# A state-space mixer with a token MLP: eight rows of x in a place of their own, loaded early, and a new order

## Chip, cores, metric

One core of a Trainium2 chip runs the whole program. The metric is the device time of one execution in microseconds; the time of before is the median of three runs. The engines are PE (matmuls), DVE and ACT (elementwise work and evictions of PSUM), POOL (small elementwise work, and transfers issued by software), SP (issues transfers). They run their own queues in order and wait for each other through semaphores.

## What is computed

The input x is `A_q`, with 2048 positions (S) and 448 channels (D). A position is split as 16 q + r, so that each of 128 partitions q holds 16 "rows" r.

```python
h  = x + A(layernorm(x), A_k, A_v, shift_k, ssm_k, ssm_D)
h2 = h + B(layernorm(h), w1, b1, w2, b2)
# A: kv = causal 4-tap filter of k along S, times v
#    y  = causal convolution of kv with ssm_k along S (FFT of length 2 S) + kv * ssm_D
#    returns layernorm(x) * y
# B: token MLP: LayerNorm again, then along S: gelu(h^T w1 + b1) w2 + b2
```

## The kernel before

The FFTs are built as two matmul stages with a shuffle in between. Everything is listed ahead of time: the emitting functions record operations, and the table `ORDER` says in which order each engine's queue takes them. An operation is named by tag, step and number: `u1.8:0-7` are the eight matmuls of the step u1.8, `u1.8:8` its eviction, 9 to 11 its shuffle transfers. The scheduler puts the waits in, and it picks the PSUM banks and ring slots by itself, the one that it reckons free first.

The stages in order of time:

- Tables, loads of the filter k, of v and of `A_k`, then the filter stage: `kv` (short filter, multiplied into V at L998 on DVE), `k1` and `u1` (first FFT stage of filter and of kv, L1050). Four steps make a group. Each step is evicted from two PSUM banks by ACT or DVE (L1058, L1060) into one of four ring slots; transfers shuffle a pair of steps into TK or TU (L1066: two on POOL, one on SP).
- `k2` and `u2` (second stage, L1085), evicted in place into TK and TU (L729 to L733).
- `i1`: 16 products on DVE (L1152, 1792 elements each), which need all shuffles landed because they write where ring slots 0 and 1 lie; matmuls (L1169), evictions (L729) and shuffles into TZ (L1193; the last step's at L1180).
- `ct`: transposes of a table (L1099). `i2`: for each row r two matmuls (L1292) and, for rows 0 and 1, four more that read TU in place (L1300). Rows 0 to 3 are combined with a normalised x that `xn` makes (L1262); the others are first evicted by a gate (L1309 on ACT, L1311 on DVE) and then combined (L1319). The combination of rows 0 to 3 is L1329.
- The second LayerNorm: statistics of the combined rows (L1335, L1338 for rows 0 and 1, squares on ACT at L1347 and sums for the others), POOL's small steps (L1357 to L1367) and its power (L1371), and the normalised row on DVE (L1378), which is the MLP's input.
- `mlp`: seven accumulations over the 16 rows (L1425), seven more with the other half of w1 (L1435), gelu (L1415), then 16 rows of 14 matmuls with w2 (L1447), sums on DVE (L1450) and stores.

The statistics of x for the first LayerNorm (`q`) are a BN statistic and an aggregate on DVE for each row (L1229, L1231) and an add and a power on POOL for two or four rows (L1237, L1240). q.1 holds rows 0 and 1, q.2 rows 2 and 3, and so on to q.8. x is loaded by four transfers of four rows (`xload`, L906, 448 KB each) into the place of ring slots 2 and 3:

```python
o_GR = (o_WR, o_WR + 8 * DB, o_X, o_X + 8 * DB)
```

so all four wait until every u shuffle has landed (`after=shuf["u"]`). On SP they stand behind the zero fill of TZ (`ct0.1:0`, L1109), which waits for POOL's memset of EW (L1125).

Of the kernel before, what the change touches and what calls it, by code (L numbers as in the profile page):

```python
# [7 lines left out]
ALU = mybir.AluOpType  # L8
# [71 lines left out]
    ),  # L80
# [8 lines left out]
    ),  # L89
}  # L90

def _hpush(h, item):
    h.append(item)
    i = len(h) - 1
    while i > 0:
        parent = (i - 1) >> 1
# [1413 lines left out]
```

## Time and profile before

| | |
|---|---|
| median of 3 runs | 173.48 us (173.15 to 174.06) |
| the profiled execution | 173.96 us, of which the span is 172.1 |
| PE busy | 161.1 us (94%), 1419 matmuls |
| DVE busy | 103.0 us (60%) |
| ACT busy | 89.5 us (52%) |
| POOL busy | 59.6 us (35%) |
| moved by DMA | 35.15 MB, mean 204 GB/s |

An engine's line gives its busy time; in section 2 of the page each digit is the busy tenth of a 4.3 us slice. DVE has 6 to 9 tenths in the first 20 slices and at most 3 in the last 10. The granted TensorE clock is full in every slice. Rows of the timeline give start, time, engine, line, operation, and in brackets the idle time ahead of it with what ended it. Rows of neighbouring operations overlap by up to a tenth of a microsecond, so lengths do not add up to the time from the first start to the last end.

### The profile page before, as it was taken

The numbers are of one execution on the slowest core, as the hardware profiler recorded it, in microseconds if no ns is written. First come the engines' busy times: TensorE is split into PE (matmuls) and PEld (weight loads), VectorE is DVE, ScalarE is ACT, GpSimd is POOL, SyncE is SP. The second block draws the span as 40 slices with busy tenths as digits, with TensorE's granted clock in tenths as the row PEclk, the third lists the DMA queues.
The fourth block names the chain that finished last, engine by engine and source line by source line (L and its number), as shares of the span: only waits on it lengthen the run. The fifth ranks groups of instructions, "written<-read, shape, count | busy, mean of one in ns | idle before, by whom it ended". The sixth has DMA issues, their size and how long they took to land.

```text
span 172.1 us, 3566 instructions
## 1 busy us (share of the span) xinstructions
PE 161.1 (94%) x1419; PEld 92.6 (54%) x1419; DVE 103.0 (60%) x191; ACT 89.5 (52%) x129; POOL 59.6 (35%) x154
## 2 busy tenths in 40 slices
PE   6999999989989988877999999999999999999994
PEld 2776745442333332433445555555567777777783
DVE  7998999868979999989897750000003132132231
ACT  3696757799999999889874447321210000000000
POOL 8346718681902524495889630000000000000000
PEclk9999999999999999999999999999999999999999
DMA  5999866792849985557999999920000111101111
GB/s 176 396 299 388 279 187 238 297 340 96 262 108 372 335 262 181 149 159 247 391 400 404 418 421 422 422 85 0 0 0 4 53 53 53 53 0 57 53 53 53
DMA packets 15404, 35.15 MB, mean 204 GB/s; under 512 B 3756, under 2 KB 9500, under 8 KB 15388
## 3 DMA queue, kind: packets, MB, share of 16 engines
q1 hardware_dynamic: 12300, 28.29, 45.3%
q0 software_dynamic: 2944, 6.55, 11.7%
q8 instruction: 11, 0.18, 0.4%
q10 hardware_dynamic: 144, 0.08, 0.2%
q14 instruction: 5, 0.04, 0.1%
HBM read 22.05 MB, written 1.84 MB: 139 GB/s over the span
## 4 chain that ended last, share of the span: by engine, by line
PE 60%; DVE 15%; DMA 10%; POOL 5%; ACT 4%; issue 2%; SPq 1%; DVEq 0%; ACTq 0%; POOLq 0%
PE ps L1447 24%; PE ps L1435 12%; PE ps L1425 12%; DVE arena L1152 9%; DMA arena<-arena 5%; DMA arena<-in_A_ssm_k_dram 5%; POOL arena L1066 3%; ACT arena L1060 3%; PE ps L1050 3%; DVE arena L1229 2%; PE ps L983 2%; PE ps L1085 2%; PE ps L1029 2%; PE ps L1292 1%; PE ps L957 1%
## 5 line engine op out<-in xcount | busy, mean ns | idle before, releaser
L1450 DVE SCALAR_TENSOR_TENSOR arena<-ps,arena 128x448 bf16<-128x448 f32 (+2 forms) x17 | 11.1, 656 | 55.7 <-PE ps L1447 55.7
L1447 PE MATMUL ps<-arena 128*128 128x448 bf16 (+2 forms) x238 | 42.7, 342 | 0.0
L1447 PEld LDWEIGHTS ps<-arena 128*128 128x128 bf16 x238 | 33.3, 145 | 9.5
L729 ACT CAST arena<-ps 128x896 bf16<-128x896 f32 (+1 forms) x31 | 24.9, 949 | 1.0 <-DVE arena L1231 0.3
L1425 PE MATMUL ps<-arena 128*128 128x448 bf16 x112 | 23.0, 353 | 1.2 <-DVE arena L1367 0.9
L1060 ACT CAST arena<-ps 128x896 bf16<-128x896 f32 x23 | 19.5, 913 | 6.0 <-PE ps L1050 5.4
L1066 POOL DMA_DIRECT2D arena<-arena x32 | 17.6, 553 | 12.5 <-ACT arena L1060 11.9
L1435 PE MATMUL ps<-arena 128*128 128x448 bf16 x112 | 21.7, 352 | 0.0
L1085 PE MATMUL ps<-arena 128*64 128x448 bf16 x128 | 15.8, 360 | 2.0 <-ACT arena L1060 0.9
L1415 ACT ACTIVATE arena<-ps,arena 128x448 bf16<-128x448 f32 x14 | 8.2, 639 | 17.5 <-PE ps L1435 15.1
L1152 DVE TENSOR_TENSOR arena<-arena 128x1792 bf16<-128x1792 bf16 x16 | 16.6, 1082 | 1.1 <-DMA arena<-arena 1.1
L1425 PEld LDWEIGHTS ps<-arena 128*128 128x128 bf16 x112 | 10.6, 98 | 12.3 <-DVE arena L1378 1.8
L1435 PEld LDWEIGHTS ps<-arena 128*128 128x128 bf16 x112 | 11.0, 98 | 10.2
L1169 PE MATMUL ps<-arena 64*128 64x448 bf16 x128 | 14.4, 351 | 1.9 <-DVE arena L1152 1.2
L1050 PE MATMUL ps<-arena 128*32 128x448 bf16 x256 | 14.8, 355 | 0.3
L1193 POOL DMA_DIRECT2D arena<-arena x15 | 8.7, 585 | 15.8 <-ACT arena L729 15.8
L1347 ACT ACTIVATE arena<-arena 128x448 bf16<-128x448 f32 x14 | 8.0, 575 | 7.0 <-DVE arena L1319 6.8
L1085 PEld LDWEIGHTS ps<-arena 128*64 128x64 f16 x128 | 5.4, 108 | 11.5 <-ACT arena L729 3.8
L1169 PEld LDWEIGHTS ps<-arena 64*128 64x128 f16 x128 | 5.1, 94 | 11.0 <-ACT arena L729 5.3
L732 DVE COPY arena<-ps 128x1024 bf16<-128x1024 bf16 (+2 forms) x15 | 9.2, 649 | 0.6 <-PE ps L1029 0.6
L1229 DVE BATCH_NORM_STATS2 arena<-arena 128x6 f32<-128x448 bf16 x16 | 9.3, 612 | 0.0
L1050 PEld LDWEIGHTS ps<-arena 128*32 128x32 f16 x256 | 5.1, 95 | 7.8 <-DVE arena L998 1.9
(97 smaller groups left out, 189.7 us busy)
## 6 DMA issues: line engine op xcount, KB each, us to landing
arena<-in_B_w_dram SPq DMA_DIRECT2D x8, 896.0 KB, 10.2
arena<-in_B_w_dram SPq DMA_DIRECT2D x2, 2048.0 KB, 17.3
arena<-arena SPq DMA_DIRECT2D x16, 224.0 KB, 3.4
arena<-arena POOLq DMA_DIRECT2D x32, 112.0 KB, 3.4
arena<-in_B_w_dram SPq DMA_DIRECT2D x2, 1536.0 KB, 19.3
arena<-arena POOLq DMA_DIRECT2D x14, 196.0 KB, 5.2
arena<-in_A_k_dram SPq DMA_DIRECT2D x4, 448.0 KB, 5.9
arena<-in_A_v_dram SPq DMA_DIRECT2D x4, 448.0 KB, 8.7
```

The costliest lines, as they stand in the source:

```text
L729: return e.copy(out=dst(), in_=src())
L1050: op("pe", lambda e, W, b=b, r=r, q=q, x=x, c0=c0: e.matmul(PS[32 * q:32 * q + 32, b.slots[x], 0:D], E[:, 2 * r + x, c0:c0 + 32], src[:, r ...
L1060: return e.copy(out=dst, in_=Ppair(b)) if W == "act" else e.tensor_copy(out=dst, in_=Ppair(b))
L1066: shuf[tag].append(op(q_, lambda e, W, g=g, i=i, a=a, nu=nu, jh=jh: e.dma_start(T[a + i:a + i + 4 * nu - 3:4].rearrange("p (j k) c d -> p ...
L1085: op("pe", lambda e, W, b=bs[h], h=h, j=j, c=c, par=par: e.matmul(PS[64 * par:64 * par + 64, b.slots[c], 0:D], FW[:, 64 * c:64 * c + 64], ...
L1152: op("dve", lambda e, W, m=m, i=i: e.tensor_tensor(out=MR(m.slots[0]).rearrange("p (x y) d -> p x y d", x=2), in0=TU[:, i].unsqueeze(2).br ...
L1169: k = op("pe", lambda e, W, b=bs[h], m=ms[h], par=par, t=t, tab=tab, xy=xy, P=P: e.matmul(Pb(b, par), tab[P, :], MR(m.slots[0])[P, xy, :], ...
L1229: op("dve", lambda e, W, bs=bs, r=r: e.bn_stats(out=bs, in_=X[:, r, :]), r=[(o_X + r * DB, DB)], w=[(ob, 24)], n=D, kind="1x")
L1425: op("pe", lambda e, W, r=r, fc=fc, b=bs[fc]: e.matmul(Pb(b), W1A[:, r, 128 * fc:128 * fc + 128], Q[:, r, :], start=(r == 0), stop=(r == R ...
L1435: op("pe", lambda e, W, r=r, fc=fc, b=b: e.matmul(Pb(b), W1B[:, r, 128 * (fc - n0):128 * (fc - n0) + 128], Q[:, r, :], start=(r == 0), sto ...
L1447: op("pe", lambda e, W, r=r, fc=fc, b=b, d0=d0, d1=d1: e.matmul(Pb(b)[:, d0:d1], W2[fc // 7][:, fc % 7, r:S:R], G[:, fc, d0:d1], start=(fc ...
L1450: op("dve", lambda e, W, r=r, b=b, A=A, d0=d0, d1=d1: e.scalar_tensor_tensor(out=X[:, r, d0:d1], in0=Pb(b)[:, d0:d1], scalar=bm[:, r:r + 1 ...
```

## The change

Rows 0 to 7 of x get a place of their own (XA, 7168 bytes in each partition at the end of the arena); rows 8 to 15 stay where ring slot 3 lies (XB). The small area shrinks from 4096 to 4032 bytes. The two loads of rows 0 to 7 no longer wait for the u shuffles and are issued on SP behind the fourth k shuffle; the other two follow after the last u shuffle, as before. The four in-place matmuls of rows 0 and 1 (L1300) come before their two other matmuls (L1292) in the accumulation. The tables `ORDER` for all engines are new, and PSUM banks and ring slots are no longer picked but written down (`SLOTS`).

```diff
-    NSMALL = 4096
+    NSMALL = 4032
...
-        TOT = SMALL + NSMALL
+        o_XA = SMALL + NSMALL
+        TOT = o_XA + 8 * DB
...
-        X = view(o_X, [R, D])
+        XA = view(o_XA, [8, D])
+        XB = view(o_X + 8 * DB, [8, D])
+        X2 = lambda r, n: (XA if r < 8 else XB)[:, r % 8:r % 8 + n]
+        XR = lambda r: (XA if r < 8 else XB)[:, r % 8, :]
+        oX = lambda r: o_XA + r * DB if r < 8 else o_X + r * DB
...
         def emit_xload():
             for c in range(4):
-                op("sp", lambda e, W, c=c: e.dma_start(X[:, 4 * c:4 * c + 4, :], x2d[:, 4 * c:4 * c + 4, :]),
-                   w=[(o_X + 4 * c * DB, 4 * DB)], dmab=128 * 4 * DB,
-                   after=shuf["u"])
+                op("sp", lambda e, W, c=c: e.dma_start(X2(4 * c, 4), x2d[:, 4 * c:4 * c + 4, :]),
+                   w=[(oX(4 * c), 4 * DB)], dmab=128 * 4 * DB, after=shuf["u"] if c > 1 else ())
...
-                    for h in range(2):
-                        k = op("pe", ... Pb(b), ET[:, 2 * r + h, :], TZ[:, r, h, :], start=(h == 0), stop=(h == 1 and r >= NZ)) ...
                     if r < NZ:
-                        sch.t0 += 0.2
                         for h in range(2):
                             for jx in range(2):
...
+                                    Pb(b), EW[:, 4 * r + 2 * jx + h, :], TU[:, j, h, :], start=(h == 0 and jx == 0), stop=False),
...
+                        sch.t0 += 0.2
+                    for h in range(2):
+                        k = op("pe", ... Pb(b), ET[:, 2 * r + h, :], TZ[:, r, h, :], start=(h == 0 and r >= NZ), stop=(h == 1)) ...
...
+SLOTS = (
+        ... k1.7:0:6 u1.7:0:2 u1.8:0:4 u1.9:0:6 u1.8:8:3 k1.3:0:4 k2.0:0:0 k2.1:0:6 k2.12:0:2 k2.13:0:4 ...
+)
...
         def can_acquire(o):
...
+            return all(turn[b.pool, i][0] is b and b.pool.free_t[i] <= t + 1e-6 for b in o.acq for i in b.slots)
```

A SLOTS entry is step, operation and bank (or slot): k1.3 gets the pair of banks 4 and 5 that u1.8 had; before it had the pair of k1.7.

What moves in the queues, in the parts that the prediction speaks of (DVE and SP from the diff, shortened to the span):

```diff
 dve:
-k1.0:8 k1.1:8 u1.3:8 kv.13:28-29 kv.14:24-25 k1.2:8 kv.15:28-29 u1.7:8 k1.3:8 k2.1:5 k2.5:4 kv.16:24-25 k2.9:5 u1.10:8 u1.11:8 k2.3:4 k2.7:4 k2.11:4 k2.15:5 u2.13:5
+k1.0:8 k1.1:8 q.2:0 kv.13:28-29 q.2:2 kv.14:24-25 q.2:3 q.2:1 q.4:2 k1.2:8 q.4:3 q.1:2 kv.15:28 q.1:0 kv.15:29 q.1:1 u1.9:8 k1.3:8 k2.1:5 k2.13:5 q.4:0 kv.16:24-25 k2.9:5 u1.12:8 q.4:1 q.1:3 q.3:2 u1.15:8 k2.3:4 k2.7:4 k2.11:5 k2.15:4 u2.13:5 u2.1:5
-i1.0:0 i1.1:0 i1.14:0 i1.13:0 i1.7:0 i1.8:0 i1.10:0 i1.9:0 q.1:0 q.1:2 q.1:1 q.2:0 q.3:0 i1.11:0 i1.12:0 ct0.0:8 q.3:1 i1.5:0 q.5:0 i1.6:0 q.5:1 u2.3:4 i1.3:0 i1.2:0 q.7:0 i1.15:0 i1.16:0
+i1.0:0 i1.1:0 i1.14:0 i1.13:0 i1.8:0 i1.7:0 xn.3:1 i1.9:0 i1.10:0 u2.11:4 q.3:0 i1.11:0 q.3:1 i1.12:0 ct0.0:8 i1.5:0 i1.6:0 i1.3:0 i1.6:9 i1.2:0 i1.16:0 i1.15:0
+q.6:2 q.3:3 q.5:0 q.6:3 q.5:2 xn.0:1 q.8:2 q.5:3 q.6:0 q.5:1 q.6:1 q.7:2 q.8:0 q.8:3 ct.0:8 q.8:1 i2.3:0 i2.11:0 i2.4:0 i2.12:0 i2.5:0 i2.13:0 i2.6:0 i2.14:0 i2.18:0 i2.21:0 i2.8:0 i2.34:0 i2.29:0 i2.16:0
 sp:
+... k1.13:11 k1.15:11 xload.0:0 xload.1:0 u1.1:11 ... u1.15:11 ct0.1:0 xload.2:0 xload.3:0 w1a.0:0 ...
 pool:
+... k1.3:9 q.2:4 k1.3:10 ... u1.11:10 ew.0:1-2 q.1:4 ew.0:3 q.1:5 ew.0:0 q.2:5 xn.0:0 xn.3:0 i1.1:19 ...
 pe:
+... i1.16:10-17 i1.16:1-8 warm.0:0 ct.0:0-7 ct.1:0-7 ct.2:0-7 i2.9:0-3 i2.1:0-3 warm.1:0 i2.2:0-1 i2.10:0-1 i2.45:0-1 ...
```

(i2.1 and i2.9 are the in-place matmuls of rows 0 and 1, i2.2 and i2.10 their other two; i2.3 and i2.11 their combinations, i2.8 and i2.16 their normalised rows.) ACT takes u1.3, u1.7, u1.10 and u1.11 and gives u1.9, u1.12 and u1.15 to DVE; its u1.7 now stands behind u1.8. In the MLP the single matmuls of rows 4 to 15 are interleaved in another way, and three of the w1 second-half accumulations (mlp.19, mlp.20, mlp.21) start between the last rows instead of mlp.17 alone. The rest of ORDER is new in the same sense, and names of x in L1229, L1262, L1319, L1450 and the stores follow the new place.

More of the change, by code (lines that the diff above doesn't have):

```diff
@@ L358, in schedule @@
         INF = 1e18
-        def can_acquire(o):
-            need = {}
-            for b in o.acq:
-                need[b.pool] = need.get(b.pool, 0) + b.k
-            for p, k in need.items():
-                if pick(p, k) is None:
-                    return False
-            return True
-        def pick(p, k):
-            ok = [x <= t + 1e-6 for x in p.free_t]
-            if k == 1:
-                best = None
-                for i in range(p.n):
-                    if ok[i]:
-                        key = (p.pairs and ok[i ^ 1], p.free_t[i], i)
-                        if best is None or key < best:
-                            best = key
-                return None if best is None else [best[2]]
-            best = None
-            for i in range(0, p.n, 2):
-                if ok[i] and ok[i + 1]:
-                    key = (max(p.free_t[i], p.free_t[i + 1]), i)
-                    if best is None or key < best:
-                        best = key
-            return None if best is None else [best[1], best[1] + 1]
+        turn = {}
+        for token in SLOTS.split():
+            step, k, i = token.split(":")
+            (b,) = ops[steps[step][int(k)]].acq
+            b.slots = [int(i) + x for x in range(b.k)]
+            for x in b.slots:
+                turn.setdefault((b.pool, x), []).append(b)
+        def can_acquire(o):
+            return all(turn[b.pool, i][0] is b and b.pool.free_t[i] <= t + 1e-6 for b in o.acq for i in b.slots)
         while done < n:
@@ L399, in schedule @@
                         p = b.pool
-                        b.slots = pick(p, b.k)
                         for i in b.slots:
+                            turn[p, i].pop(0)
                             b.extra.extend(p.prev[i])
@@ L1228, in emit_q @@
                     bs = view(ob, [6], f32)
-                    op("dve", lambda e, W, bs=bs, r=r: e.bn_stats(out=bs, in_=X[:, r, :]), r=[(o_X + r * DB, DB)],
+                    op("dve", lambda e, W, bs=bs, r=r: e.bn_stats(out=bs, in_=XR(r)), r=[(oX(r), DB)],
                        w=[(ob, 24)], n=D, kind="1x")
@@ L1261, in norm @@
                         if W == "act":
-                            return e.activation(out=XN[:, r, :], in_=X[:, r, :], func=ACT.Identity, bias=qx[:, r, 1:2],
+                            return e.activation(out=XN[:, r, :], in_=XR(r), func=ACT.Identity, bias=qx[:, r, 1:2],
                                                 scale=qs[:, r, 3:4])
-                        return e.tensor_scalar(out=XN[:, r, :], in0=X[:, r, :], scalar1=qs[:, r, 0:1],
+                        return e.tensor_scalar(out=XN[:, r, :], in0=XR(r), scalar1=qs[:, r, 0:1],
                                                scalar2=qs[:, r, 3:4], op0=ALU.subtract, op1=ALU.mult)
-                    op(FX, norm, r=[(o_X + r * DB, DB), (o_qst + 16 * r, 16), (o_qx + 8 * r, 8)],
+                    op(FX, norm, r=[(oX(r), DB), (o_qst + 16 * r, 16), (o_qx + 8 * r, 8)],
                        w=[(o_TK + r * 4 * D, 4 * D)], n=D, est={"act": 664.0, "dve": 430.0})
@@ L1290, in emit_i2 @@
                     tz = [(o_TZ + r * 2 * DB, 2 * DB)]
-                    for h in range(2):
-                        k = op("pe", lambda e, W, b=b, r=r, h=h: e.matmul(
-                            Pb(b), ET[:, 2 * r + h, :], TZ[:, r, h, :], start=(h == 0), stop=(h == 1 and r >= NZ)),
-                           r=[r_ET(r)] + tz, bw=[b], n=D, after=av[-1:] if r >= 8 and h == 0 else ())
                     if r < NZ:
-                        sch.t0 += 0.2
                         for h in range(2):
@@ L1300, in emit_i2 @@
                                 k = op("pe", lambda e, W, b=b, r=r, h=h, j=j, jx=jx: e.matmul(
-                                    Pb(b), EW[:, 4 * r + 2 * jx + h, :], TU[:, j, h, :], start=False, stop=(h == 1 and jx == 1)),
-                                   r=[(o_EW + 1024 * r + 512 * jx + 256 * h, 256), (o_TU + (2 * j + h) * DB, DB)], bw=[b], n=D, safter=(k,))
+                                    Pb(b), EW[:, 4 * r + 2 * jx + h, :], TU[:, j, h, :], start=(h == 0 and jx == 0), stop=False),
+                                   r=[(o_EW + 1024 * r + 512 * jx + 256 * h, 256), (o_TU + (2 * j + h) * DB, DB)], bw=[b], n=D,
+                                   safter=(k,) if h + jx else ())
+                        sch.t0 += 0.2
+                    for h in range(2):
+                        k = op("pe", lambda e, W, b=b, r=r, h=h: e.matmul(
+                            Pb(b), ET[:, 2 * r + h, :], TZ[:, r, h, :], start=(h == 0 and r >= NZ), stop=(h == 1)),
+                           r=[r_ET(r)] + tz, bw=[b], n=D, after=av[-1:] if r >= 8 and h == 0 else (),
+                           safter=(k,) if r < NZ else ())
                     i2_last.append(k)
@@ L1318, in comb @@
                     def comb(e, W, r=r, A=A, acc=None):
-                        return e.scalar_tensor_tensor(out=A, in0=X[:, r, :], scalar=qs[:, r, 0:1], in1=A,
+                        return e.scalar_tensor_tensor(out=A, in0=XR(r), scalar=qs[:, r, 0:1], in1=A,
                                                       op0=ALU.subtract, op1=ALU.mult,
                                                       **({} if acc is None else {"accum_out": acc}))
-                    rx = tz + [(o_X + r * DB, DB), (o_qst + 16 * r, 16)]
+                    rx = tz + [(oX(r), DB), (o_qst + 16 * r, 16)]
                     bx = []
@@ L1450, in emit_mlp @@
                     op("dve", lambda e, W, r=r, b=b, A=A, d0=d0, d1=d1: e.scalar_tensor_tensor(
-                        out=X[:, r, d0:d1], in0=Pb(b)[:, d0:d1], scalar=bm[:, r:r + 1], in1=A[:, d0:d1], op0=ALU.add, op1=ALU.add),
-                       r=[(o_bm, 64), (o_TZ + r * 2 * DB, 2 * DB)], w=[(o_X + r * DB + 2 * d0, 2 * (d1 - d0))], br=[b],
+                        out=XR(r)[:, d0:d1], in0=Pb(b)[:, d0:d1], scalar=bm[:, r:r + 1], in1=A[:, d0:d1], op0=ALU.add, op1=ALU.add),
+                       r=[(o_bm, 64), (o_TZ + r * 2 * DB, 2 * DB)], w=[(oX(r) + 2 * d0, 2 * (d1 - d0))], br=[b],
                        n=d1 - d0, kind="psum")
                     if r == R - 1:
-                        op("sp" if d0 else "act", lambda e, W, r=r, d0=d0, d1=d1: e.dma_start(o2d[:, r:r + 1, d0:d1], X[:, r:r + 1, d0:d1]),
-                           r=[(o_X + r * DB + 2 * d0, 2 * (d1 - d0))], dmab=128 * 2 * (d1 - d0), rate=400.0)
+                        op("sp" if d0 else "act", lambda e, W, r=r, d0=d0, d1=d1: e.dma_start(o2d[:, r:r + 1, d0:d1], X2(r, 1)[:, :, d0:d1]),
+                           r=[(oX(r) + 2 * d0, 2 * (d1 - d0))], dmab=128 * 2 * (d1 - d0), rate=400.0)
                 if r % 2 == 1 and r < 14:
-                    op("sp", lambda e, W, r=r: e.dma_start(o2d[:, r - 1:r + 1, :], X[:, r - 1:r + 1, :]),
-                       r=[(o_X + (r - 1) * DB, 2 * DB)], dmab=128 * 2 * DB, rate=400.0)
+                    op("sp", lambda e, W, r=r: e.dma_start(o2d[:, r - 1:r + 1, :], X2(r - 1, 2)),
+                       r=[(oX(r - 1), 2 * DB)], dmab=128 * 2 * DB, rate=400.0)
                 elif r == R - 2:
-                    op("sp", lambda e, W, r=r: e.dma_start(o2d[:, r:r + 1, :], X[:, r:r + 1, :]),
-                       r=[(o_X + r * DB, DB)], dmab=128 * DB, rate=400.0)
+                    op("sp", lambda e, W, r=r: e.dma_start(o2d[:, r:r + 1, :], X2(r, 1)),
+                       r=[(oX(r), DB)], dmab=128 * DB, rate=400.0)
         PLAN = (("dummy", emit_dummy, ()), ("tables", emit_tables, ()), ("loads", emit_loads, ()), ("kv", emit_kv, ()), ("kT", emit_kT, ()),
```

140 rows, old and new, of tables (ORDER, SLOTS) are left out of this document.

## The prediction

> **What bounds the kernel now.** I read the shares of the chain first, then the chain in order of time, then the windows by stage, and last the timelines of DVE and PE where the chain runs through them. The page and its chain:
>
> ```profile
> span 172.1 us, 3566 instructions
> ...
> PE 60%; DVE 15%; DMA 10%; POOL 5%; ACT 4%; issue 2%; SPq 1%; DVEq 0%; ACTq 0%; POOLq 0%
> ```
>
> No single engine sets the end. In order of time the chain is: a shuffle's landing, DVE's products, a second half-serial stretch, and then PE without a break:
>
> ```profile
> 28.92 4.93 DMA arena<-arena
> ...
> 45.54 4.23 DMA arena<-arena
> ...
> 49.85 1.10 DVE arena L1152
> ...
> 83.61 1.50 PE ps L1425 x7
> ```
>
> The windows (PE, PEld, DVE, ACT, POOL busy; clock; DMA share; GB/s) say how full each stretch is:
>
> ```profile
> 25.00:27.00 2.00, 1.94 (x46) 0.91 (x40) 1.95 (x3) 1.75 (x3) 0.77 (x2) 1.00 0.00 0
> ...
> 28.00:40.00 12.00, 10.95 (x200) 5.27 (x196) 9.84 (x14) 10.48 (x13) 7.94 (x15) 1.00 0.85 320
> 51.00:54.00 3.00, 2.71 (x26) 1.05 (x28) 3.00 (x4) 3.00 (x5) 0.00 (x0) 1.00 0.97 341
> ```
>
> ```profile
> 26.80:49.80 23.00, 21.20 (x320) 9.04 (x314) 19.07 (x23) 20.06 (x24) 14.02 (x27) 1.00 0.69 243
> ```
>
> Three readings matter: the DMA engines stand still from 25 to 27 us; DVE has 23.00 - 19.07 = 3.9 us of idle time in the filter stage; and a window from 83.6 to 169.3 has PE busy 85.69 of 85.70 us. So whatever brings the first MLP matmuls forward brings the end forward, as long as PE stays full. PE's last pauses are these:
>
> ```profile
> 75.09 0.54 PE L1292 MATMUL ps<-arena 128*128 128x448 bf16 x2 [1.23 <-DMA arena<-arena]
> ...
> 81.39 0.55 PE L1425 MATMUL ps<-arena 128*128 128x448 bf16 x2 [0.90 <-DVE arena L1367]
> ...
> 83.61 1.50 PE L1425 MATMUL ps<-arena 128*128 128x448 bf16 x7 [0.35 <-DVE arena L1378]
> ```
>
> And among the products DVE also makes statistics of x, which no product needs:
>
> ```profile
> 58.00 1.14 DVE L1229 BATCH_NORM_STATS2 arena<-arena 128x6 f32<-128x448 bf16 x2
> 59.06 0.17 DVE L1231 BATCH_NORM_AGGREGATE arena<-arena 128x2 f32<-128x6 f32 x1
> 59.14 1.12 DVE L1229 BATCH_NORM_STATS2 arena<-arena 128x6 f32<-128x448 bf16 x2
> ```
>
> Neighbours overlap a little in these rows, so I use the distance from start to start: statistics 0.54 us, aggregate 0.09, product 1.0, an eviction of two banks 1.0 on DVE and 0.80 on ACT.
>
> **The early x loads.** Two loads of 0.46 MB are issued on SP behind the fourth k shuffle, at about 21.55 us; they wait for nothing. Cost on SP: two issues at 0.43, while SP's next shuffle waits for ACT until 25.97, so nothing there. On the DMA engines: 0.92 MB at 341 GB/s is 2.7 us. The 25 to 27 gap gives 2.0, and the window from 21.5 to 25 has a DMA share of 0.77, another 0.8: it just fits. When the first load lands matters more, since row 2's statistics stand at DVE's head at 26.8 with the filter's multiplies (L998) queued behind. The four x loads of before took 3.2 to 6.7 us to land (median 5.0): 24.8 to 28.3, and I take 26.6, no wait. The upper end costs 1.5.
>
> **The filter stage gets 0.6 us longer.** DVE takes in seven statistics and six aggregates, 7 x 0.54 + 6 x 0.09 = 4.3 us; five evictions leave it (u1.3, u1.7, u1.10, u1.11 and one of k2) and five come (u1.9, u1.12, u1.15 and one each of k2 and u2). 4.3 against 3.9 us of idle time is +0.4 at least. Behind the statistics, the eviction of k1.2 goes from 30.3 to 30.8 and that of k1.3 from 34.1 to 35.4, the latter also because its matmuls now have the banks of u1.8, which ACT frees only at 34.8 (its wait for the 4.93 us landing). u1.7's eviction moves behind u1.8's on ACT, so POOL issues its shuffle at 35.6 instead of 34.7, and all behind it on POOL by 0.8 to 1.0. Walking on with the same steps, the last shuffle is issued at 46.05 instead of 45.54 and lands 4.23 later, at 50.3; DVE reaches the first product at 50.45, before 49.85. POOL's added small operations (one add among the shuffles, two powers of 0.7 ahead of the memset of EW) move the zero fill on SP from 47.75 to 49.4; the late x loads behind it wait until 50.3 for the shuffles anyway.
>
> **The products get 1.85 us shorter.** Five of six statistics (2.7 us) and two of three aggregates inside the run go; one eviction more comes in (i1.6, 1.0), u2.11 replaces u2.3, xn adds 0.07. From first product to the end of the last: before 21.2, after 19.35, so 69.8 instead of 71.05. For ACT it is 28 evictions instead of 30; from u2.13 at 48.1 it needs 28 x 0.80 = 22.4, to 70.5, so it isn't the bound. The last product's matmuls (0.93) and eviction (0.9) then end at 71.8, before 72.98: -1.2.
>
> **From there to the MLP.** Between last product and the first combination (L1329) DVE had 6.0 us: eight statistics, a table copy, small ones, 0.5 waiting for POOL. Now: 7 x 0.54 + 7 x 0.09 + 0.08 + 0.6 = 5.0, so 74.8 instead of 77.06. On the other side PE waits there for the shuffle of i1.4. Its eviction ends at 70.1 instead of 70.83 and the landing goes from 74.89 to 74.2. The eight in-place matmuls (L1300, 8 x 0.19 = 1.5 us) no longer stand between that landing and rows 0 and 1: they run at 72.2, in the 1.23 us pause. Two matmuls on, row 0 is there at 75.0. So the first combination starts at 75.0: -2.05. Then DVE: four combinations at 0.6, two statistics, six small ones, 3.9 us, as before: the normalised row 0 starts at 78.9 (before 80.84) and its first MLP matmul at 79.4. Row 1 had to wait for POOL's power of 82.00 to 83.00, because DVE's variance step for it (81.24) stood behind the write of row 0 and POOL's power behind a step of rows 2 and 3; now both variances and both powers come first, and DVE writes row 1 after two more steps, at 80.5 to 81.0. The seven matmuls of row 1 start at 81.1 instead of 83.61: -2.5. Rows 2 and 3 (82.65, 84.35) come just ahead of PE (82.8, 84.5), so I give 0.2 back.
>
> **Sum.** Filter +0.6, products -1.85, stretch to row 0 -0.8, row 1's pause -0.45, jitter +0.2: -2.3 us. The MLP's reordering on PE changes no count, and its weights are issued about a microsecond earlier: nothing. The profiled execution took 173.96 (span 172.1 and 1.86 around it), 0.48 above the median of 173.48; 173.96 - 2.3 = 171.66 there, and **171.2 us** against the median. About 0.5%, 0.87 us, is what a measurement here can tell from no change.
>
> **Rival 1: the pause doesn't hold the x loads (slower).** The place is 21.6 to 34 us. If the loads run into the shuffles of 27 to 40, where 320 GB/s is all that is moved, 0.92 MB costs 2.9 us, in the landing that ACT waits for at 33.91, and everything behind it. If row 2 lands as late as the slower x loads of before (6.05), DVE's queue is held for another 0.9. Together 3.8 against 2.3: 175.0. It turns slower by 0.5% once the two add up to 3.2, seen as u1.8's eviction starting after 37.1. For it: the loads fit with 0.1 to spare, and DVE has no idle time left to take a late row in. Against: 0 GB/s from 25 to 27, and the k shuffles still under way at 21.6 have landed by 25.05, about 2 us before anyone needs them. The Trainium skill (DMA: Bandwidth & Descriptors, Issuing engines are not separate DMA queues) says that transfers issued by different engines run on the same 16 DMA engines and interleave. By that rule any overlap is paid by POOL's shuffles as well as SP's, so the sum goes toward this rival's 175.0. The trace agrees so far as it shows it: the third and fourth x load, which met each other and the first weight load, took 6.05 and 6.66 us to land, the first 3.22.
>
> **Rival 2: the gain is lost again ahead of PE (no change).** Rows 6 and 7 were written by DVE until 91.26 and PE took row 6 at 91.45, so the later rows were only 0.2 ahead. If ACT's squares and POOL's powers keep them where they were, PE starts earlier and waits the gain away: 173.3. Against: every input of those rows comes earlier by 1 to 2 us, DVE has one statistic less in between, and PE needs 18 x 0.19 = 3.4 us for a pair of rows (14 MLP and 4 inverse matmuls), DVE 2 x 0.6 + 2 x 0.45 = 2.1.
>
> **Rival 3: the filter stage takes the statistics for nothing.** If DVE's waits there come from PE and the added work fits between them, the first product stays at 49.85: 170.6.
>
> **Chances.** The forecast with its spread (0.6 either side, from the x landing and the 4 to 5 us shuffle landings) 0.50, rival 3 0.10, rival 2 0.15, rival 1 0.25. Rival 2 is divided: 0.03 of it is still faster, the rest no change; 0.03 of rival 1 stays there too. So faster 0.63 (0.50 + 0.10 + 0.03), same 0.15, slower 0.22. The forecast's own range is 170.6 to 171.8. The whole range reaches from 170.2 to 174.9: below lies only what rival 3 could add, above the worst of rival 1.
>
> **What would show it.** Right: the first product near 50.4; its run near 19.4 us with one statistic in it; no PE pause on a DMA after the in-place matmuls longer than 1 us; the first MLP row near 79.4, row 1 near 81.1, PE full behind. Wrong: DVE held at L1229 by a DMA near 27; ACT's wait for a DMA ending past 34.5; the first product past 51.5; or pauses at the MLP's rows 2 to 7.

## The result, and the profile after

| | median | ratio to before, 95% interval |
|---|---|---|
| before | 173.86 us (22 runs) | |
| after, first set | 172.92 us (22 runs) | 0.9928, 0.9908 to 0.9949 |
| after, second set (e1) | 172.36 us (6 runs) | 0.9884, 0.9857 to 0.9910 |
| after, third set (e13) | 172.69 us (7 runs) | 0.9906, 0.9871 to 0.9941 |

By the ratios the kernel is faster, by 1.25 us in the first set, 2.0 in the second and 1.6 in the third; the mean of the three ratios, 0.9906, is 1.6 us. The forecast was 2.3 us. The ratios leave out executions more than 1.5% above the fastest (six of the first set's 22, among them one of 902.32 us and the profiled one of 175.87), and since losses of the kernel itself are among these, the ratios flatter it: the medians of all executions of the first set are only 0.94 us apart. I read the profile of e13 (171.74 us, span 169.9), the execution without a loss, and use the first one (span 174.1) to show what can go wrong.

In all kernels here the engines' work ahead of the eviction of k1.0 on DVE is the same (the early loads of x are issued ahead of it on SP), and yet this eviction starts anywhere from 24.05 to 25.81 us. So profiles are compared from there on. In us, from one execution each:

| kernel | DVE held for x | k1.0 to first product | products | last product to MLP | of it from the first combination | last shuffle's landing | k1.0 to the last w2 row |
|---|---|---|---|---|---|---|---|
| before | - | 25.18 | 21.20 | 10.34 | 4.33 | 4.0 | 142.06 |
| e2, in-place first | - | 25.25 | 21.19 | 10.34 | 4.33 | 4.0 | 142.13 |
| e3, early loads | - | 25.12 | 21.20 | 10.33 | 4.32 | 4.0 | 142.25 |
| after, first profile | 1.57 | 27.12 | 19.78 | 11.67 | 6.59 | 5.0 | 143.81 |
| after, e1 | 0.44 | 25.61 | 19.73 | 10.02 | 4.88 | 4.8 | 140.65 |
| after, e13 | 0 | 25.17 | 19.73 | 9.85 | 4.45 | 4.3 | 139.98 |
| e4, late statistics | 0 | 26.89 | 19.72 | 9.75 | 4.45 | 4.4 | 141.59 |
| e5, PE filled | 0 | 25.25 | 19.73 | 9.91 | 4.45 | 4.4 | 140.12 |
| e6, x one place later | 0 | 26.10 | 19.72 | 10.22 | 5.22 | 5.0 | 141.48 |
| e7, statistics back | - | 25.35 | 25.26 | 11.76 | 4.41 | 4.8 | 147.71 |
| e8, in-place last | 0.74 | 25.92 | 19.73 | 11.11 | 4.99 | 5.0 | 142.15 |
| e9, x earlier | 0 | 25.64 | 19.73 | 10.29 | 5.01 | 5.1 | 140.94 |
| e10, x earlier, filled | 0 | 25.59 | 19.73 | 10.32 | 4.96 | 5.1 | 141.07 |
| e11, x later | 4.54 | 30.89 | 19.78 | 9.77 | 4.44 | 4.4 | 145.82 |
| e12, small last shuffle | 0 | 25.80 | 19.78 | 10.22 | 4.45 | 3.8 | 141.03 |

"Held" is the time for which DVE waits for x at row 2's first statistic, called the hold below ("-" where that statistic isn't there). "Products" is from the start of the first to the end of the last; "MLP" is its first matmul; the landing is from issue to arrival of i1.16's shuffle; the last column ends at the start of the last row. The kernel before and its two variants (e2, e3) agree within 0.2 us in the last column. The changed kernel, unmodified, reads 139.98, 140.65 and 143.81: from 2.1 us faster to 1.7 slower. So there is no single size to explain, but a gain of 2.1 us without losses, and losses that come in some executions.

The execution without losses (e13), its chain:

```profile
PE 60%; DVE 12%; ACT 11%; POOL 7%; DMA 5%; issue 4%; DVEq 0%; POOLq 0%; ACTq 0%
```

Windows (PE, PEld, DVE, ACT, POOL busy; clock; DMA share; GB/s): the gap of 25 to 27 us in e13, then the filter stage from k1.0's eviction to the first product, before and in e13:

```profile
25.00:27.00 2.00, 1.94 (x50) 1.05 (x44) 1.95 (x3) 2.00 (x4) 0.90 (x2) 1.00 0.90 337
...
24.68:49.85 25.17, 23.27 (x360) 9.90 (x353) 21.14 (x25) 22.18 (x27) 14.59 (x28) 1.00 0.63 222
...
24.54:49.71 25.17, 23.39 (x362) 10.21 (x356) 24.96 (x39) 22.63 (x28) 16.70 (x34) 1.00 0.72 257
```

The gap of 25 to 27 us, 0 GB/s before, now carries 337. The filter stage is as long as before, 25.17 us, with DVE busy for 24.96 us of it in place of 21.14: the change brought 3.8 us of work into 4.0 us of idle time. Rows of e13's DVE timeline, at the head of the statistics (no wait) and around the last product:

```profile
26.68 0.62 DVE L1233 BATCH_NORM_STATS2 arena<-arena 128x6 f32<-128x448 bf16 x1
...
66.11 3.32 DVE L1156 TENSOR_TENSOR arena<-arena 128x1792 bf16<-128x1792 bf16 x3
...
74.84 1.27 DVE L1335 SCALAR_TENSOR_TENSOR arena<-ps,arena 128x448 f32<-128x448 f32 x2 [0.50 <-PE ps L1305]
```

And PE's timeline of e13, with the in-place matmuls (L1299) ahead of the others (L1305):

```profile
71.89 1.68 PE L1299 MATMUL ps<-arena 128*128 128x448 bf16 x8
...
74.26 0.92 PE L1305 MATMUL ps<-arena 128*128 128x448 bf16 x4 [0.50 <-issue]
76.07 2.81 PE L1305 MATMUL ps<-arena 128*128 128x448 bf16 x14 [0.89 <-DMA arena<-arena]
79.28 0.55 PE L1431 MATMUL ps<-arena 128*128 128x448 bf16 x2 [0.41 <-DVE arena L1384]
...
92.62 3.01 PE L1431 MATMUL ps<-arena 128*128 128x448 bf16 x15 [0.30 <-DVE arena L1384]
```

The first MLP matmul stands at 79.28 (before 81.39), row 1 follows without a pause, and there is one new pause of 0.30 in the MLP. In the execution profiled first, DVE's timeline shows waits that e13 does not have, one for x in the filter stage and others at the combinations of rows 2 and 3 (the longer one):

```profile
28.65 0.63 DVE L1233 BATCH_NORM_STATS2 arena<-arena 128x6 f32<-128x448 bf16 x1 [1.57 <-DMA arena<-in_A_q_dram]
...
80.76 0.68 DVE L1335 SCALAR_TENSOR_TENSOR arena<-ps,arena 128x448 f32<-128x448 f32 x1 [1.18 <-ACT arena L1315]
```

PE's timeline and the windows of that execution say why the later ones came:

```profile
79.07 4.43 PE L1305 MATMUL ps<-arena 128*128 128x448 bf16 x14 [1.89 <-DMA arena<-arena]
```

```profile
79.00:82.00 3.00, 2.93 (x8) 1.17 (x9) 1.27 (x7) 1.22 (x2) 1.06 (x2) 0.50 0.53 152
82.00:85.00 3.00, 3.00 (x16) 1.35 (x14) 2.75 (x8) 3.00 (x8) 1.56 (x5) 0.94 1.05 400
```

After a pause of 1.89 us for i1.16's shuffle the clock is 0.50 from 79 on; fourteen matmuls take 4.43 us in place of 2.81.

### The profile page after: what moved, and what is told of

Its sections match the earlier page's. It is cut to its first block, busy times and chain, and to the rows that moved or that the text cites. A ratio compares the mean times of both kernels' runs of the same rounds, so it can differ in the third digit from the quotient of the medians.

```text
span 174.1 us, 3570 instructions
## 1 busy us (share of the span) xinstructions
PE 162.2 (93%) x1419; PEld 94.3 (54%) x1419; DVE 104.2 (60%) x192; ACT 88.6 (51%) x128; POOL 60.0 (34%) x154
## 3 DMA queue, kind: packets, MB, share of 16 engines
HBM read 22.05 MB, written 1.84 MB: 137 GB/s over the span
## 4 chain that ended last, share of the span: by engine, by line
PE 58%; ACT 13%; DMA 9%; DVE 8%; POOL 6%; issue 4%; DVEq 0%; POOLq 0%; ACTq 0%
PE ps L1453 24%; PE ps L1441 12%; DMA arena<-arena 9%; ACT arena L734 9%; PE ps L1431 6%; PE ps L1020 3%; PE ps L961 3%; PE ps L1054 2%; PE ps L1033 2%; ACT arena L1064 2%; PE ps L1305 2%; DVE arena L1002 2%; PE ps L1173 2%; POOL arena L1070 2%; POOL arena L1377 1%
## 5 line engine op out<-in xcount | busy, mean ns | idle before, releaser
L1431 PE MATMUL ps<-arena 128*128 128x448 bf16 x112 | 23.8, 353 | 0.3 <-DVE arena L1384 0.3
L734 ACT CAST arena<-ps 128x896 bf16<-128x896 f32 (+1 forms) x29 | 23.3, 901 | 1.2 <-PE ps L1173 0.4
L1064 ACT CAST arena<-ps 128x896 bf16<-128x896 f32 x24 | 20.3, 914 | 6.3 <-PE ps L1054 6.2
L1441 PE MATMUL ps<-arena 128*128 128x448 bf16 x112 | 22.5, 352 | 0.0
L1089 PE MATMUL ps<-arena 128*64 128x448 bf16 x128 | 15.1, 360 | 1.3 <-ACT arena L735 0.5
L1305 PE MATMUL ps<-arena 128*128 128x448 bf16 x32 | 9.1, 413 | 2.1 <-DMA arena<-arena 1.9
```

Of the source, the lines that this page charges most:

```text
L734: return e.copy(out=dst(), in_=src())
L1064: return e.copy(out=dst, in_=Ppair(b)) if W == "act" else e.tensor_copy(out=dst, in_=Ppair(b))
L1089: op("pe", lambda e, W, b=bs[h], h=h, j=j, c=c, par=par: e.matmul(PS[64 * par:64 * par + 64, b.slots[c], 0:D], FW[:, 64 * c:64 * c + 64], ...
L1305: k = op("pe", lambda e, W, b=b, r=r, h=h: e.matmul(Pb(b), ET[:, 2 * r + h, :], TZ[:, r, h, :], start=(h == 0 and r >= NZ), stop=(h == 1)) ...
L1431: op("pe", lambda e, W, r=r, fc=fc, b=bs[fc]: e.matmul(Pb(b), W1A[:, r, 128 * fc:128 * fc + 128], Q[:, r, :], start=(r == 0), stop=(r == R ...
L1441: op("pe", lambda e, W, r=r, fc=fc, b=b: e.matmul(Pb(b), W1B[:, r, 128 * (fc - n0):128 * (fc - n0) + 128], Q[:, r, :], start=(r == 0), sto ...
```

## The experiments

Three theories stood after the first profile. A: the early load of x lands late in some executions and holds DVE. B: the filter stage is over-full with the statistics, whatever the load does. C: the gain is lost at the inverse stage, in the wait for i1.16's shuffle and the half clock behind it.

**e1, the changed kernel again.**

> The changed kernel unchanged, for a profile of an execution with a full TensorE clock. Theory A (the early x load lands too late: DVE is held at row 2's statistics): the hold is there too, 1.0 to 1.7 us at L1233, x's first load lands at 28.0 to 28.7, the first product stands at 51.5 to 52.0. Theory B (the filter stage is over-full whatever the load does): the hold is under 0.5 us and the first product is past 51.3 all the same. Theory C (what is missing is lost at the inverse stage, in PE's wait for the shuffle of i1.16 and the half clock behind it): the first product is near 50.4 and PE waits over 1.5 us near 77. Time 172.3 to 172.9 us.

Ratio 0.9884. A hold of 0.44 us; the first product 25.61 us behind k1.0's eviction, at 49.66; PE's pause 1.66 us, at full clock. The hold is shorter than A's 1.0 to 1.7 us, and C's pause is there. B in its first form (past 51.3 us whatever the load does) falls already here: with a hold of 0.44 the stage is 0.43 longer than before.

**e2, one part alone: in-place matmuls first, in the kernel before.**

```diff
-ct.0:0-7 ct.2:0-7 i2.1:0-1 i2.2:0-3 i2.9:0-1 i2.10:0-3 i2.28:0-1
+ct.0:0-7 ct.2:0-7 i2.1:0-3 i2.9:0-3 i2.2:0-1 i2.10:0-1 i2.28:0-1
```

(with the emitting code as changed)

> The kernel before with one part of the change alone: the in-place matmuls of rows 0 and 1 stand ahead of their two other matmuls. By the prediction's step they fill the pause of 1.23 us before the landing of i1.4, and rows 0 and 1 leave PE 1.0 to 1.3 us earlier; but DVE comes to the first combination from its statistics only at about 76.6 (77.06 with PE's wait), so the time falls by 0.4 at most: 173.0 to 173.6 us. If PE's order is what holds the first combination, it falls by 1.0: 172.5. If the wait for the shuffle of i1.16 simply takes the place of the pause, nothing changes, within 0.2.

Ratio 0.9997 (0.9967 to 1.0027): nothing. PE's pause moves from i1.4's landing to 1.26 us ahead of the rows behind 0 and 1, and the stretch to the MLP stays 10.34: DVE, busy with statistics, sets the first combination.

**e3, another part alone: the place and the early loads, in the kernel before.**

```diff
-k1.15:11 u1.1:11 ... ct0.1:0 xload.2:0 xload.1:0 xload.3:0 xload.0:0 w1a.0:0
+k1.15:11 xload.0:0 xload.1:0 u1.1:11 ... ct0.1:0 xload.2:0 xload.3:0 w1a.0:0
```

> The kernel before with the new place for rows 0 to 7 and their two loads issued behind the fourth k shuffle; all statistics and all other queues as before. It gives the price of the transfers alone, without statistics on DVE. Theory A: DVE does not wait for x, the shuffles have slack, so the first product stays within 0.4 of 49.85 and the time within 0.4 of before (173.2 to 174.0). The rival (the loads push the shuffles of 25 to 34 us, and everything behind them): the first product past 50.8 and the time at 174.5 or more.

Ratio 1.0006 (0.9982 to 1.0030), first product 25.12 us behind k1.0. The median shuffle of the filter stage lands in 3.9 us in place of 3.4, but the products start no later. The rival's price for the 0.92 MB, 2.9 us, is not there: the shuffles have that slack.

**e4, the statistics later on DVE.**

```diff
-q.2:0 kv.13:28-29 q.2:2 kv.14:24-25 q.2:3 q.2:1 q.4:2 k1.2:8 q.4:3 q.1:2 kv.15:28 q.1:0 kv.15:29 q.1:1 u1.9:8
+kv.13:28-29 kv.14:24-25 k1.2:8 q.2:0 q.2:2 kv.15:28 q.2:3 kv.15:29 q.2:1 q.4:2 q.4:3 q.1:2 q.1:0 q.1:1 u1.9:8
```

> The changed kernel, with only DVE's order changed: the statistics of rows 2, 3, 7, 1, 0 stand behind the multiplies of kv.13 and kv.14 and the eviction of k1.2, where x has landed for sure. Theory A: no wait for x, k1.2's eviction at 29.5 to 30.5 instead of 32.6, the first product 1.0 to 1.6 earlier than in the changed kernel (50.4 to 50.9), time 171.0 to 171.6 us. Theory B: the 4.3 us of statistics only come later, the first product moves by less than 0.4, time 172.2 to 172.8. Theory C: the first product may move, the time does not.

All three were wrong: slower, ratio 1.0086 (1.0055 to 1.0117). No hold, and yet the first product is at 26.89, 1.7 us later than in e13. DVE's timeline of e4 says why:

```profile
28.33 1.29 DVE L1002 TENSOR_TENSOR arena<-ps,arena 128x512 bf16<-128x512 f32 x2 [0.51 <-PE ps L987]
29.97 1.02 DVE L1002 TENSOR_TENSOR arena<-ps,arena 128x512 bf16<-128x512 f32 x2 [0.36 <-PE ps L987]
31.23 1.09 DVE L1062 TENSOR_TENSOR arena<-ps,arena 128x896 bf16<-128x896 f32 x1 [0.24 <-PE ps L1054]
```

Three waits for PE, 1.1 us in all, are idle again; the statistics come when there is no idle time left and push u1.9 and k1.3. So a narrower B holds: the statistics are free only in the places where DVE waits for PE.

**e6, x's first statistic one place later.**

```diff
-q.2:0 kv.13:28-29 q.2:2 kv.14:24-25 q.2:3 q.2:1
+kv.13:28-29 q.2:0 kv.14:24-25 q.2:2 q.2:3 q.2:1
```

> The changed kernel with row 2's first statistic one place later on DVE, behind the multiplies of kv.13 instead of ahead of them, and row 3's behind kv.14. Theory A (x's landing between 26.7 and 28.7 holds DVE in part of the executions): no wait of DVE for x over 0.3 us in the profile, first product within 0.3 of 25.6 us behind the first eviction of k1.0 (the changed kernel: 25.6 without and 27.1 with the long hold), time 171.9 to 172.4. Rival (the hold of 1.6 us was one odd execution, and the place is as good as the other): time within 0.3 of the changed kernel.

Ratio 0.9962 (0.9929 to 0.9995), 173.97 us: slower than either expected. No hold, but 26.10 to the first product: the wait of 0.51 us for PE ahead of kv.13, which row 2's statistic had filled, is back. So the place is a choice between that wait and the risk of a late x.

**e11, the suspected cost made larger: x one shuffle later on SP.**

```diff
-k1.15:11 xload.0:0 xload.1:0 u1.1:11 k1.1:11
+k1.15:11 u1.1:11 xload.0:0 xload.1:0 k1.1:11
```

> The changed kernel with both early loads of x issued one shuffle later on SP, behind u1.1's, which waits for ACT until 25.3: x lands about 4.5 us later, near 31. Theory A (a hold of DVE at row 2's statistics goes one to one into the end): hold 4 to 5 us, first product 29 to 30 us behind k1.0's eviction, time 176 to 177.5. Rival (DVE makes up for the hold further on, where the stage waits for shuffles): time under 175.

Ratio 1.0267 (1.0224 to 1.0310), 178.83 us, longer than expected. The hold, on DVE, and PE, which ran dry behind it:

```profile
31.54 0.63 DVE L1233 BATCH_NORM_STATS2 arena<-arena 128x6 f32<-128x448 bf16 x1 [4.54 <-DMA arena<-in_A_q_dram]
```

```profile
33.41 1.18 PE L1054 MATMUL ps<-arena 128*32 128x448 bf16 x16 [3.80 <-DVE arena L1002]
```

The first product is 5.7 us later than in e13 for a hold of 4.54 us: nothing of it is made up, and it grows by a quarter. The clock falls there too (0.74 in the window of 33 to 35 us, 0.60 from 35 to 38), which an expectation of one to one left out.

**e9, x's first load one shuffle sooner.**

```diff
-k1.13:11 k1.15:11 xload.0:0 xload.1:0 u1.1:11
+k1.13:11 xload.0:0 k1.15:11 xload.1:0 u1.1:11
```

> The changed kernel with the first early load of x issued one shuffle sooner on SP (behind the third k shuffle, about 1.6 us earlier, in SP's wait for k1.15), the second behind the fourth. Theory A (only x's landing makes the changed filter stage longer; the statistics themselves fit): the hold of DVE at row 2's statistics is 0 to 0.3 us, the first product stands 25.2 to 25.4 us behind k1.0's eviction, as in the kernel before (25.1 to 25.3), and the median falls by 0.3 to 0.7 against the changed kernel. Rival (the earlier load takes what the k shuffles had, so k1.0's eviction or the u shuffles come later): no hold, but the first product at 25.6 or more and no gain.

Ratio 0.9896 (0.9847 to 0.9944), not to be told from the changed kernel's. The hold is gone, but the first product is at 25.64: ACT waits 0.6 us for a shuffle and k1.3's matmuls come 0.36 late. The rival's half of it came true.

**e7, a part undone: the early statistics back among the products.**

```diff
-q.2:0 kv.13:28-29 q.2:2 kv.14:24-25 q.2:3 q.2:1 q.4:2 k1.2:8 q.4:3 q.1:2 kv.15:28 q.1:0 kv.15:29 q.1:1 u1.9:8
+kv.13:28-29 kv.14:24-25 k1.2:8 kv.15:28-29 u1.9:8
...
-u2.11:4 q.3:0
+u2.11:4 q.2:0 q.2:2 q.2:3 q.2:1 q.4:2 q.4:3 q.1:2 q.1:0 q.1:1 q.3:0
...
-i1.15:0 q.6:2
+i1.15:0 q.4:0 q.4:1 q.1:3 q.3:2 q.6:2
```

> The changed kernel with the statistics of rows 0 to 3 and 5 to 7 taken out of the filter stage: five statistics and four aggregates back among the products, the others behind the last product, POOL's and ACT's steps for them where they were before; loads, banks and all else as changed. By the prediction's steps the filter stage gets 0.4 shorter, the products 5 x 0.54 + 4 x 0.09 = 3.1 longer, the stretch behind them 2 x 0.54 + 2 x 0.09 = 1.3 longer: 175.5 to 177.0 us. If the filter stage pays for the statistics what the products save (theory B), the time is within 0.6 of the changed kernel.

Ratio 1.0302 (1.0261 to 1.0342), 179.49 us, 2.5 above the upper end. (POOL's and ACT's steps for these rows moved back as well.) The filter stage is 0.2 longer than in e13 although thirteen operations left it (those of the diff's first line and the four put behind the last product), so it pays nothing for them. The products take 25.26 us, 5.5 more and not 3.1: PE ran dry behind the statistics, which with q.3:0 stand in one block of ten operations (before, at most five in a row), and ran at half clock after that (timeline and window of e7):

```profile
65.23 1.67 PE L1173 MATMUL ps<-arena 64*128 64x448 bf16 x8 [2.79 <-DVE arena L1156]
```

```profile
65.20:68.00 2.80, 2.77 (x16) 0.98 (x16) 2.80 (x5) 0.91 (x1) 0.00 (x0) 0.50 0.25 84
```

**e8, another part undone: in-place matmuls last.**

```diff
-i2.9:0-3 i2.1:0-3 warm.1:0 i2.2:0-1 i2.10:0-1
+warm.1:0 i2.1:0-1 i2.2:0-3 i2.9:0-1 i2.10:0-3
```

(with the emitting code of before)

> The changed kernel with the in-place matmuls of rows 0 and 1 behind their two other matmuls, as before. The first combination then waits for four more matmuls: it starts at about 75.3 instead of 74.5. If rows 0 and 1 set the MLP's start, the time rises by 0.5 to 0.8 (172.9 to 173.5); if rows 2 and 3, which wait for the shuffle of i1.16 until 76.5, set it, it stays within 0.2, and the pause before them shrinks from 1.66 to about 0.2, so that no execution shows the lower clock.

173.35 us, ratio 0.9974 (0.9938 to 1.0010), as expected if rows 0 and 1 set the start of the MLP. DVE's first combination waits for PE in e8's timeline, and the stretch to the MLP is 11.11 us:

```profile
77.58 0.68 DVE L1333 SCALAR_TENSOR_TENSOR arena<-ps,arena 128x448 f32<-128x448 f32 x1 [1.21 <-PE ps L1304]
78.72 0.68 DVE L1333 SCALAR_TENSOR_TENSOR arena<-ps,arena 128x448 f32<-128x448 f32 x1 [0.45 <-PE ps L1304]
```

The same edit that was worth nothing in e2 is worth about 1 us here (11.11 against 9.85 to 10.02), because the statistics that kept DVE busy in e2 are gone and it now waits for these matmuls.

**e5, the pause before i1.16's shuffle filled.**

```diff
-i2.10:0-1 i2.45:0-1
+i2.10:0-1 warm.2:0 warm.3:0 warm.4:0 warm.5:0 warm.6:0 warm.7:0 warm.8:0 i2.45:0-1
```

(warm.2 to warm.8 are idle matmuls; their number N_WJ goes from 2 to 9)

> The changed kernel with seven more idle matmuls (0.19 us each, 1.3 us in all, results unused) on PE between rows 0 and 1 and rows 8 and 9, that is in PE's pause of 1.66 us before the shuffle of i1.16 lands. Theory C (the pause with its rare drop of the TensorE clock to half is what is missing): the mean granted clock is 0.998 or more in every execution, none is at 0.99, and the median falls by 0.2 to 0.4, since 5 of 28 executions of the changed kernel had the drop at 1.5 to 2 us each. If the pause itself, not the clock, is what costs, the executions at 0.99 go and the median stays within 0.2 of the changed kernel's 172.4 to 172.9. If the drop has another cause, executions at 0.99 are still there.

Ratio 0.9915 (0.9879 to 0.9952), no better than the changed kernel's 0.9906; the gain of 0.2 to 0.4 us did not come. **e10, both** (e5's and e9's edits together):

> Both: x's first load one shuffle sooner and the seven idle matmuls in PE's pause before the shuffle of i1.16 lands. If theory A and theory C both hold and add up, this is the fastest version: no execution below a mean clock of 0.998, time 171.5 to 172.2, ratio to before 0.984 to 0.989. If the clock's drop is not set by the pause, executions at 0.99 are still there.

172.56 us, ratio 0.9907 (0.9877 to 0.9938), where 0.984 to 0.989 was expected: no faster than the changed kernel's 0.9906, so the best version that these runs pointed to is not a better one. For the clock they agree with C: an execution at a mean clock of 0.99 or less comes 5 times in 35 of the changed kernel as it is, and 0 in 20 of e5 and e10. If the fill changed nothing, such a split would still come about once in ten times; and without a fill there are 4 in 12 of e6 and 4 in 6 of e4, but 1 in 12 of e8 and none in 6 of e9. So the counts alone are weak evidence (the last section has a better one). Nor is the clock all: three of e5's ten executions took 174.0 to 175.5 us at full clock, and why is not shown.

**e12, the last shuffle relieved.** The two large transfers of i1.4 are issued early with other rows as their source.

```diff
-for g_, a, b_, j0 in (("zpool", 0, 112, 0), ("zsp", 112, 128, 14)):
+for g_, a, b_, j0 in (("zpool", 0, 112, 0), ("zsp", 112, 128, 14))[jj == 1:]:
...
-i1.10:22 ct0.1:2
+i1.10:22 y.0:0 ct0.1:2
```

(and `y.0:1` behind `i1.10:21` on POOL)

> The changed kernel with the two large transfers of i1.4's shuffle (196 KB each) taken out of the end of the inverse stage: they are issued some 8 us earlier with the rows of another step as their source, so the numbers in TZ are not the reference's and only the time is read. i1.16's shuffle then has the DMA engines nearly to itself. Theory C (the last shuffle lands late because i1.4's lies 1.6 us ahead of it, 2.15 before; DVE's combination of rows 2 and 3 and so the MLP waits for it): it lands 3.0 to 4.0 us after its issue instead of 4.4 to 5.1, DVE does not wait at i2.18, the stretch from the end of the last product to the first MLP matmul is 9.6 to 9.8 us instead of 9.9 to 10.3, no execution shows 0.99, and the median is 0.2 to 0.6 below the changed kernel's of this call. Rival (the landing has its length by itself): 4.4 us or more as before, and no change of the time.

**e13, the changed kernel beside it.**

> The changed kernel unchanged, beside the one above on the same chip: 172.0 to 173.2 us, 0.987 to 0.993 of before; hold of DVE at row 2's statistics 0 to 1.6 us; first product 25.2 to 25.7 us behind k1.0's eviction plus 1.2 times the hold; stretch from the last product to the first MLP matmul 9.9 to 10.3 us unless the clock drops.

e13 came about as expected: 172.69 us, no hold, 25.17 and 9.85 us. In e12 i1.16's shuffle lands in 3.8 us and DVE does not wait at rows 2 and 3 (4.45 us from the first combination to the MLP), none of 12 executions shows the lower clock; but the time is the same, ratio 0.9914 (0.9883 to 0.9945), and the stretch to the MLP is 10.22 us, not 9.6 to 9.8. Its PE timeline (lines nine higher) shows that the edit brought a wait of its own, inside the in-place matmuls:

```profile
74.79 1.50 PE L1308 MATMUL ps<-arena 128*128 128x448 bf16 x7 [0.85 <-DMA arena<-arena]
```

The copies of a table into EW, behind the early transfer on SP, came late. So that i1.4's transfers lengthen the last landing is shown by this profile (3.8 against 4.3 to 5.1); what a shorter landing is worth in time is not.

## Why the prediction was right or wrong

**Direction and whole range held, the size did not**: 171.2 was forecast, with 170.6 to 171.8 as its own range, and 172.4 to 172.9 measured. Without losses the kernel comes near it (e13: 2.08 us less than before from k1.0 on, against 2.3). What failed are two waits that the sum put at nothing: DVE's for the first x load, and that of rows 2 and 3 for the shuffle of i1.16. Two of the prediction's own signs showed both: a hold near 27 us, and a PE pause on a DMA longer than 1 us behind the in-place matmuls (1.66 in e1, 1.89 in the first profile).

**Early loads: wrong in "no wait".** The landing taken, 26.6, is what e1 shows (26.7), but it is 28.63 in the first profile, beyond the bound of 28.3. The hold was 0, 0.44, 0.74 and 1.57 us in executions with this place, and goes into the first product one to one (0.44 and 0.74), with about a quarter more where it is long (1.57 and 4.54). This is the largest loss in both profiles of the changed kernel that have one, and the prediction had it as the upper end of a range and not in its sum. In all of these executions the load is issued 3.1 us ahead of k1.0's eviction; from issue to landing it takes 4.79 us in e13, 5.75 in e1 and 6.88 in the first profile. Its issue on SP was mis-sized too (0.59, 0.99 and 1.15 us, not 0.43). Why the landing differs so stays open.

**The filter stage, +0.6: wrong, 0.0 in e13.** The sum set 4.3 us of work against 3.9 of idle time, took the rest as lost and let the later evictions push the shuffles. In the traces it is 3.8 against 4.0 (24.96 less 21.14, and 25.17 less 21.14), so the work fits by a hair, and the stage keeps its length with DVE busy 99%. Rival 3 (the statistics for nothing) was right for this step; e4 and e6 show how narrowly, 0.9 to 1.7 us when the places move.

**The products, -1.85: mis-sized, -1.42 to -1.47 in the three profiles.** The counts were right. 0.23 us is a new wait ahead of the product i1.16 (67.07 to 67.30 in e1), which the trace puts down to an ACT eviction (L734); the rest is rounding: the five statistics and two aggregates that left cost 2.80 by their starts, where 2.88 was taken.

**From the last product to the MLP, -0.8 in the sum (-0.74 by its own times, 10.34 to 9.6): wrong, -0.49 in e13, -0.32 in e1 and +1.33 in the first profile.** The first combination came at 5.1 to 5.4 us behind the last product, where 5.0 was forecast on DVE (its own terms add up to 5.09) and 5.2 on PE. From it to the MLP 4.4 us were forecast, and 4.45 is what all profiles of the new order show in which the last shuffle lands within 4.4 us of its issue. Where it takes 4.8 to 5.1, the combination of row 2 waits and it is 4.88 to 5.22 (6.59 with the half clock; e7, where DVE comes 2 us later, does not wait). The step that failed is that rows 2 and 3 were not followed to their own input: i1.16's shuffle, issued 1.6 us behind i1.4's and no longer 2.15.

**Row 1, -0.45: right**, -0.52: 1.71 us behind row 0 in e13, before 2.23. **The MLP, +0.2: 0.40** in e13, of which 0.30 is the pause at 92.62.

In sum, e13: 0.0 - 1.47 - 0.49 - 0.52 + 0.40 = -2.08. That this is near 2.3 is in part luck: the loss of 0.6 forecast in the filter stage did not come, and the products, the stretch to the MLP and the MLP came out 0.4, 0.3 and 0.2 worse than forecast. What e1 and the first profile lose against e13 (0.67 and 3.83 us) is the hold with what follows from it (0.44 and 1.95) and, for nearly all the rest, the stretch to the MLP (0.17 and 1.82, with the landing and the clock). The other executions were not profiled, so how much of the shortfall of the medians each of these makes is not shown; nor does any run take the hold away and leave the rest as it is, since e9 and e10, without a hold, reach the first product 0.4 to 0.5 us later than e13.

**Rival 1** named the hold rightly, and the landing "as late as the slower x loads", but most of its price was contention, which cost nothing in e3. By the Trainium skill (DMA: Bandwidth & Descriptors, Issuing engines are not separate DMA queues) SP's and POOL's transfers interleave on the same engines; the trace agrees, since the median shuffle landing goes from 3.4 to 3.9 us, but this was no cost on the path. **Rival 2** (waits in the MLP) came as the one pause of 0.30.

## What to carry to other kernels

Work moved onto a full engine was free here where that engine waited for another, and cost 0.9 to 1.7 us where it stood later, so find those waits one by one; a sum of busy against idle time that comes out within half a microsecond does not tell whether the work fits, and never where. An operation that waits for a transfer, put at the head of a full in-order queue, makes the spread of the transfer's landing the spread of the kernel: plan with the latest landing of the traces, not a typical one, and with some room (28.63 came here where 28.3 was the bound). An edit can be worth nothing alone and a microsecond together with the one that clears the engine behind it, so undo parts from the changed kernel as well as adding them to the old one.

## What the runs showed of the hardware

Short pauses of TensorE halved its clock in three profiles: 1.89 us in the first (0.50 from 78.98 us, for 3.41 us), 3.80 in e11 (from 33.97, which is 0.56 us after PE had resumed, for 3.41), and 2.79 and 2.04 in e7 (from 64.28 for 6.83, and from 84.76 for 3.41). Pauses of 1.66 us in e1, 1.97 in e8 and 2.00 in e6 passed at full clock. The clock records of the fifteen traces tell these apart: every stretch at one clock that begins and ends inside a trace is a whole multiple of 3.413 us long (3.41 and 6.83 at half, 27.31, 71.68 and 167.25 at full: 8, 21 and 49 times), so each trace can be cut into windows of that length. These are windows at whose end the clock fell, from the first profile (PE busy 1.43 us) and e7 (1.57, 1.37), and the one with the least PE work at whose end it stayed, of e9 (1.63):

```profile
75.57:78.98 3.41, 1.43 (x7) 0.39 (x5) 3.24 (x8) 2.55 (x4) 1.69 (x3) 1.00 0.45 124
...
60.87:64.28 3.41, 1.57 (x18) 0.82 (x16) 3.27 (x10) 2.58 (x3) 1.79 (x4) 1.00 0.69 209
81.35:84.76 3.41, 1.37 (x8) 0.67 (x8) 3.41 (x12) 3.03 (x5) 2.32 (x4) 1.00 0.26 71
...
76.05:79.46 3.41, 1.63 (x10) 0.71 (x8) 3.07 (x9) 1.76 (x4) 1.02 (x3) 1.00 0.22 62
```

In these traces the clock fell whenever PE had been idle for 1.84 us or more of a window at full clock, and never with 1.78 or less (a profile's ends of matmuls are modelled, so the limit between them is rough). A pause that lies across the edge of two windows is shared between them: e6's 2.00 us gives 1.44 to one and about 0.65 to the other. And the edges lie elsewhere in each execution (the first one behind k1.0's eviction comes 0.45 us after it in e1, 2.92 in the first profile), which fits a fall in some executions only. The Trainium skill (TensorE: Matmul & The Clock Gate, What's actually happening) gives a free-running window of about 3.4 us and lets the clock fall after an idle one; the traces agree with the window and with its running freely, but one with 1.57 us of PE work was idle enough, so an idle window in full isn't needed.

Issuing a load of 0.46 MB on SP took 0.33 to 1.66 us in these profiles (e9's second early load the longest), and the same code reached k1.0's eviction anywhere within 1.8 us (24.05 to 25.81).
